# Seven products in place of eight for the last two groups of the second layer

## The chip, the cores and the metric

The kernel runs on one core of a Trainium2 chip. The metric is the device time of one execution in microseconds; lower is better. The kernel before took 1112.73 us in the median of three runs (1112.61 to 1113.55).

## The reference

```
# attention: 4 batches x 8 heads, 576 tokens, head size 64; only scores within tau of a row's maximum count
x  = attn_out.transpose(0, 2, 1, 3).reshape(2304, 512)
# first layer
h = x @ w_in1                                  # [2304, 2048]
g = where(h >= 1, h, where(h <= -1, 0, (h + 1)**2 / 4))
x = g @ w_out1                                 # [2304, 512]
# second layer
h = x @ w_in2                                  # the first product
g = h * clip(h + 3, 0, 6) / 6                  # the gate
return (g @ w_out2).astype(float32)            # the second product
```

All in float32. The change concerns the first product of the second layer alone.

## The kernel before

The tokens are taken in groups. In the second layer there are four groups of 512 tokens (0 to 3) and one of 256 (4). The 2048 hidden columns are taken in 16 blocks f of 128. Each float32 operand is split in two parts, a rounded one (hi) and the remainder (lo), and a product of two such operands takes three matmuls: hi by hi, hi by lo, lo by hi. The split of a tile is one copy on ScalarE (ACT) and one subtraction on VectorE (DVE) or GpSimd (POOL).

`dense` (L888) runs the second layer as a list of steps (group, f), 16 for each group. A step has the first product for this f (`em_h`, L710: four chunks of the 512 inputs by three terms, 12 matmuls of 512 columns, at L719), the gate (ReLU on ACT L732, minimum and product on DVE L733, copy to hi on ACT L736, remainder on POOL L737), and, two steps late (`MLAG`), the second product for the f of two steps before (`em_out`, L746: four blocks of tokens by three terms, 12 matmuls at L761, which add up over all f in a pair of PSUM banks). After the last f of a group `fin_out` (L814) copies the four blocks out, two on DVE (L819) and two on ACT (L817), and stores them. The first products turn through four PSUM banks, Q0 to Q3; the outputs use two pairs, P0 and P1. For the group of 256 tokens the first product has 256 columns and the second two blocks of tokens.

The inputs of a group come back from DRAM (`x2d`) through three buffers `xst` and are split in `split_x` (L674; L696 load, L699 hi, L700 lo); the program asks for them in steps 11 to 14 of the group before. The weights of the second layer are loaded through three buffers `w_raw` (L97, L100) and split while the first layer's last groups and group 3 run (`ahead3`, L1059); from then on all of them stay on the chip, in the tiles `wi` and `wo`. The order of the groups is 3, 0, 1, 4, 2 (L1064).

What each engine's queue holds in which order is fixed when the program is built: instructions written earlier have priority, and one that is not ready by the builder's model of time lets a later one pass. On the chip each queue runs in that order. All loads and stores here are issued from the queue of SP.

## Time and profile before

| | before |
|---|---|
| median of the runs, us | 1112.73 |
| lowest and highest run, us | 1112.61, 1113.55 |
| profiled execution, us | 1113.27 |
| its span, first to last instruction, us | 1111.5 |
| TensorE (PE) busy, us | 1080.1 |
| VectorE (DVE) busy, us | 590.5 |
| ScalarE (ACT) busy, us | 619.6 |
| GpSimd (POOL) busy, us | 449.3 |
| moved by DMA, MB | 84.26 |

Busy times are sums over the instructions of one profiled execution, the span is from its first to its last instruction, and the profiled execution's own time lies 1.8 us above the span. Every time below comes from that execution. PEld is TensorE's weight load, which overlaps with PE. A busy PE says that a matmul was under way, not that columns passed at the full rate; for the rate one counts matmuls in a stretch.

### The profile page before, as it was taken

How to read it: one execution, taken by the hardware profiler on the slowest of the kernel's cores; microseconds unless marked ns; L12 is line 12 of the kernel's file. 1: busy time of each engine (PE TensorE's matmuls, PEld its weight loads, DVE VectorE, ACT ScalarE, POOL GpSimd, SP SyncE). 2: the span in 40 equal slices, each digit the busy share in tenths (PEclk: the TensorE clock that was granted, in tenths of full speed). 3: DMA queues.
4: the chain of work that ended last, by engine and by line, in shares of the span. 5: the costliest groups of instructions: out<-in, count | busy, mean ns of one | idle time of the engine just before them, and what ended most of it. 6: DMA issues, size and time to landing. Idle time of an engine off the chain costs nothing.

```text
span 1111.5 us, 17816 instructions
## 1 busy us (share of the span) xinstructions
PE 1080.1 (97%) x6562; PEld 886.0 (80%) x6562; DVE 590.5 (53%) x1205; ACT 619.6 (56%) x1227; POOL 449.3 (40%) x390
## 2 busy tenths in 40 slices
PE   7988889999999999999999999999999999999998
PEld 5555567778888888888799888888888888898886
DVE  6889898975767766255437665557411111211111
ACT  5777886876667667455657766545422232333222
POOL 1133767732322222165627566667522222222221
PEclk9999899999999999999999999999999999999999
DMA  6455445333222120024323445433010110010001
GB/s 172 119 100 105 124 118 134 70 87 74 62 63 64 41 80 26 29 85 153 94 78 96 151 148 161 153 108 95 25 37 1 34 38 1 10 39 11 10 1 38
DMA packets 140614, 84.26 MB, mean 76 GB/s; under 512 B 99824, under 2 KB 123632, under 8 KB 140528
## 3 DMA queue, kind: packets, MB, share of 16 engines
q1 hardware_dynamic: 139184, 82.84, 27.1%
q8 instruction: 51, 0.84, 0.3%
q10 hardware_dynamic: 1344, 0.30, 0.1%
q14 instruction: 35, 0.29, 0.1%
HBM read 65.73 MB, written 17.37 MB: 75 GB/s over the span
## 4 chain that ended last, share of the span: by engine, by line
PE 79%; DVE 8%; ACT 4%; POOL 3%; issue 2%; DMA 2%; SPq 1%; DVEq 0%; POOLq 0%; ACTq 0%
PE Q L719 31%; PE P L761 25%; PE Q L781 6%; PE Q L476 6%; PE P L375 5%; PE Q L289 5%; DVE p L390 2%; DVE p L412 2%; POOL w_c L138 1%; DVE w_c L136 1%; ACT e L403 1%; SPq L228 1%; DVE r L730 1%; DVE xl L700 1%; POOL gl L737 1%
## 5 line engine op out<-in xcount | busy, mean ns | idle before, releaser
L737 POOL TENSOR_TENSOR gl<-r,gh 128x512 fp32r<-128x512 f32 (+1 forms) x190 | 204.5, 1077 | 462.4 <-ACT gh L736 451.1
L719 PE MATMUL Q<-xh,wih 128*128 128x512 f32 (+1 forms) x760 | 261.5, 344 | 2.5 <-DVE r L730 2.3
L719 PE MATMUL Q<-xl,wih 128*128 128x512 f32 (+1 forms) x760 | 256.9, 338 | 0.0
L719 PE MATMUL Q<-xh,wil 128*128 128x512 f32 (+1 forms) x760 | 256.8, 338 | 0.0
L733 DVE SCALAR_TENSOR_TENSOR r<-r,Q 128x512 f32<-128x512 f32 (+1 forms) x80 | 50.7, 634 | 249.5 <-ACT r L732 249.4
L736 ACT ACTIVATE gh<-r 128x512 fp32r<-128x512 f32 (+1 forms) x190 | 100.0, 527 | 125.3 <-PE P L761 52.2
L719 PEld LDWEIGHTS Q<-xh,wih 128*128 128x128 f32 x760 | 144.0, 189 | 25.8 <-DVE r L730 3.8
L719 PEld LDWEIGHTS Q<-xl,wih 128*128 128x128 f32 x760 | 144.0, 189 | 15.8
L719 PEld LDWEIGHTS Q<-xh,wil 128*128 128x128 f32 x760 | 143.8, 189 | 15.3
L732 ACT ACTIVATE r<-Q,three 128x512 f32<-128x512 f32 (+1 forms) x80 | 51.4, 643 | 144.1 <-PE Q L719 140.9
L412 DVE SCALAR_TENSOR_TENSOR p<-p,th,e 128x576 f32<-128x576 f32 x144 | 122.7, 874 | 16.0 <-ACT e L403 10.3
L403 ACT ACTIVATE e<-p,nm 128x576 f32<-128x576 f32 x144 | 109.4, 776 | 33.9 <-DVE p L390 33.0
L730 DVE SCALAR_TENSOR_TENSOR r<-r,Q 128x256 f32<-128x256 f32 (+1 forms) x110 | 54.9, 499 | 123.5 <-ACT r L729 118.3
L289 PE MATMUL Q<-ident,p 128*128 128x128 f32 x656 | 106.6, 280 | 9.9 <-ACT Gf L440 7.1
L761 PE MATMUL P<-woh,gh 128*128 128x512 f32 x288 | 111.9, 390 | 0.6 <-DVE ob L819 0.6
L761 PE MATMUL P<-wol,gh 128*128 128x512 f32 x288 | 112.2, 390 | 0.0
L761 PE MATMUL P<-woh,gl 128*128 128x512 f32 x288 | 111.0, 390 | 0.0
L138 POOL TENSOR_TENSOR w_c<-w_c,w_raw 128x512 int32<-128x512 int32 x64 | 89.2, 1395 | 40.8 <-DVE w_c L136 21.5
L289 PEld LDWEIGHTS Q<-ident,p 128*128 128x128 f32 x656 | 73.8, 140 | 39.0 <-ACT Gf L440 13.0
L375 PE MATMUL P<-kt,qt 64*128 64x288 f32 (+2 forms) x508 | 84.1, 418 | 11.1 <-DVE p L390 9.2
L440 ACT ACTIVATE Gf<-Q 128x512 f32<-128x512 f32 x128 | 74.3, 596 | 16.3 <-PE Q L289 15.6
L728 ACT ACTIVATE r<-Q,half 128x256 f32<-128x256 f32 (+1 forms) x110 | 58.7, 535 | 33.4 <-PE Q L719 25.1
(106 smaller groups left out, 1960.7 us busy)
## 6 DMA issues: line engine op xcount, KB each, us to landing
w_raw<-in_moe_w_in_dram SPq DMA_DIRECT2D x32, 512.0 KB
w_raw<-in_moe_w_out_dram SPq DMA_DIRECT2D x32, 512.0 KB
vn<-in_v_dram SPq DMA_DIRECT2D x32, 128.0 KB
x2p<-ob SPq DMA_DIRECT2D x16, 256.0 KB
x2d<-ob SPq DMA_DIRECT2D x16, 256.0 KB
xst<-x2d SPq DMA_DIRECT2D x16, 256.0 KB
out_dram<-ob SPq DMA_DIRECT2D x16, 256.0 KB
xst<-xd SPq DMA_DIRECT2D x15, 256.0 KB
```

The lines of the kernel that those rows point to most:

```text
L138: x = G.tensor_tensor(out=c.bitcast(I32), in0=c.bitcast(I32), in1=r, op=ALU.add)
L289: x = T.transpose(out, in_, ident)
L375: mm = T.matmul(o, a[j][r, cs], w[j][r, k0:k0 + HS], start=(n == 0), stop=(n == len(terms) - 1), skip_group_check=True)
L403: pins["S"] = S.activation(out=e, in_=p[:, x], func=ACTF.Exp, bias=nm[:, x:x + 1], scale=-1.0)
L412: pins["M"] = V.scalar_tensor_tensor(out=p[:, x], in0=p[:, x], scalar=th[:, x:x + 1], in1=e, op0=ALU.is_le, op1=ALU.mult, accum_out=zt[j][ ...
L440: S.activation(out=f[:, h, :, d0:d0 + 128], in_=tm.rearrange("p (c n) -> p c n", c=4), func=ACTF.Copy)
L476: mm = T.matmul(o[h * D:(h + 1) * D], vn[j % 2][:, c, h, :], f[:, h, c] if c < 4 else t, start=(c == 0), stop=(c == 4), skip_group_check=True)
L719: mm = T.matmul(h, l[:, kk * 128:(kk + 1) * 128], r, start=(x == 0), stop=(x == 3 * KD - 1))
L736: x = S.activation(out=gh, in_=r, func=ACTF.Copy)
L737: y = G.tensor_tensor(out=gl, in0=r, in1=f32(gh), op=ALU.subtract)
L761: T.matmul(a, l, r, start=(first and x == 0), stop=(last and x == 2))
L781: mm = T.matmul(o, l, r, start=(f == fs[0] and x == 0 and i == 0), stop=(f == fs[-1] and x == 2 and i == 1), skip_group_check=True)
```

## The change

The order of the groups becomes 3, 0 in `dense` and then a new function `unit` for groups 1 and 2 together, with group 4 (`last`) woven into its end.

`unit` takes the f in pairs. For a pair, the first product of both groups is a product of two-by-two blocks: two halves of the 512 inputs, two f, two groups of tokens. Strassen's method (in Winograd's form) takes seven products of blocks for it in place of eight. Each has two chunks by three terms, 6 matmuls of 512 columns. It needs four sums of weight blocks (S1 to S4) for each pair and four of token blocks (T1 to T4), and on the results three copies to SBUF on ACT and four sums on DVE. Three of the products add onto a bank that holds an earlier one, after that one was copied out.

`combine` makes the sums of weights, splits them in hi and lo, and stores them with the plain blocks to DRAM (`sd`), for one pair in each of the steps 1 to 8 of group 0. It holds the sums in the buffers `pb` and `w_raw`. `prepare` loads the tokens of groups 1 and 2, makes their sums and splits them, in steps 11 and 12 of group 0; the parts take the tiles `wi` of f 0 to 13. `fetch` brings the weights of each product back from DRAM, 256 KB at a time, into twelve buffers that held the inputs of a group before.

In `unit`, the gates of group 1 go on to its second product, woven between the products of the next pair (`outs`). The gates of group 2 are stored to DRAM (`rd2`) and loaded and split again after the last pair (`again`); its second product comes last. In between, group 4 gets its weights back from DRAM (`fetch_rest`) and is woven into the second product of group 2.

The diff, cut to its core:

```diff
+    sd = [dram.tile([128, 8, 2, 256], F32, name=f"sd{p}") for p in range(KF // 2)]
+    rd2 = [dram.tile([128, MAIN], F32, name=f"rr{f}") for f in range(KF)]
...
+    def place_of(f, hl, dt, name):
+        return (wbase if f < NF1 else wpool[f]).tile([128, 512], dt, tag=f"wi{hl}{f}", name=name)
...
+            wide["t"] = ctx.enter_context(tc.tile_pool(name="tx", bufs=1, side="right"))
...
+    G1, G2 = 1, 2
+    order3 = [NB - 1, 0]
+    combos = {}
+    XN = ("B11", "B21", "T2", "T3", "T4", "T1", "B22")
+    PRODUCTS = tuple(zip(("A11", "A12", "S2", "S3", "A22", "S1", "S4"), XN))
+    WN = ("A11", "A12", "A21", "A22", "S1", "S2", "S3", "S4")
+    def halves(n, name):
+        return place_of(n, "h", F32R, name), place_of(n, "l", F32R, name)
+    def temps(c):
+        if c == 0:
+            return ([wide["p"].tile([128, MAIN], F32, tag="xst", name="tx", bufs=3) for _ in range(3)]
+                    + [wide["t"].tile([128, MAIN], F32, tag=f"t{x}", name="tx") for x in range(3)])
+        return ([wide["p"].tile([128, MAIN], F32, tag="pb", name="tx", bufs=KD) for _ in range(4)]
+                + [wide["t"].tile([128, MAIN], F32, tag=f"t{x}", name="tx") for x in (3, 4)])
+    def prepare(c):
+        b11, b21, b12, b22, t1, t2 = temps(c)
+        for t, g, kk in ((b11, G1, c), (b21, G1, 2 + c), (b12, G2, c), (b22, G2, 2 + c)):
+            nc.sync.dma_start(out=t, in_=x2d[g][:, kk, :])
+        def part(k, t):
+            hi, lo = combos[c, XN[k]] = halves(2 * k + c, "xw")
+            S.activation(out=hi, in_=t, func=ACTF.Copy)
+            E = G if k % 2 else V
+            E.tensor_tensor(out=lo, in0=t, in1=f32(hi), op=ALU.subtract)
+        def minus(o, x, y):
+            V.tensor_tensor(out=o, in0=x, in1=y, op=ALU.subtract)
+        part(0, b11)
+        part(1, b21)
+        minus(t1, b12, b11)
+        minus(t2, b22, t1)
+        part(2, t2)
+        minus(b12, b22, b12)
+        part(3, b12)
+        minus(b11, t2, b21)
+        part(4, b11)
+        part(5, t1)
+        part(6, b22)
+    ring = []
+    RING = [f"x{hl}{kk}" for kk in range(3) for hl in "hl"]
+    got = {}
+    def fetch(p, w):
+        t = wide["x"].tile([128, 2, 2, 128], F32R, tag=RING[len(ring) % 6], name="sw", bufs=2)
+        ring.append(t)
+        nc.sync.dma_start(out=f32(t), in_=sd[p][:, WN.index(w)].rearrange("p x (k n) -> p x k n", k=2))
+        got[p, w] = t
+    turn_of = {}
+    def ringed(tag, dt):
+        k = turn_of[tag] = turn_of.get(tag, -1) + 1
+        first, extra = {"r": (2, ("t3", "t4")), "gh": (3, ("t1",)), "gl": (3, ("t2",))}[tag]
+        k %= first + len(extra)
+        if k < first:
+            return wide["g"].tile([128, MAIN], dt, tag=tag, name=tag, bufs=first)
+        return wide["t"].tile([128, MAIN], dt, tag=extra[k - first], name=tag)
+    def gate(src):
+        r = ringed("r", F32)
+        S.activation(out=r, in_=src, func=ACTF.Relu, bias=three)
+        V.scalar_tensor_tensor(out=r, in0=r, scalar=6.0, in1=src, op0=ALU.min, op1=ALU.mult)
+        return r
+    def parts(r):
+        gh, gl = ringed("gh", F32R), ringed("gl", F32R)
+        S.activation(out=gh, in_=r, func=ACTF.Copy)
+        G.tensor_tensor(out=gl, in0=r, in1=f32(gh), op=ALU.subtract)
+        return gh, gl
+    def outs_of(g, accs, i, f, hl):
+        if i % 2 == 0 and f == 0:
+            accs[i // 2] = pair_bank(f"P{i // 2}")
+        a = accs[i // 2][:, i % 2]
+        gh, gl = hl
+        wh, wl = wsp["o", 1, f]
+        c = slice(i * 128, (i + 1) * 128)
+        for x, (l, r) in enumerate(((gh[:, c], wh), (gh[:, c], wl), (gl[:, c], wh))):
+            T.matmul(a, l, r, start=(f == 0 and x == 0), stop=(f == KF - 1 and x == 2))
+        if f == KF - 1:
+            fin_out(g, a, i)
+    def unit():
+        accs, gg = {}, {}
+        for p in range(KF // 2):
+            def product(k, role, first=True):
+                w, x = PRODUCTS[k]
+                if (p, w) not in got:
+                    fetch(p, w)
+                t = got.pop((p, w))
+                if first:
+                    banks[role] = bank(f"Q{(p + role) % 4}")
+                y = 0
+                for c in range(2):
+                    xh, xl = combos[c, x]
+                    for l, r in ((0, xh), (0, xl), (1, xh)):
+                        T.matmul(banks[role], t[:, l, c, :], r, start=(first and y == 0), stop=(y == 5),
+                                 skip_group_check=True)
+                        y += 1
+                if p + 1 < KF // 2:
+                    fetch(p + 1, w)
+                return banks[role]
+            banks = {}
+            def copy(name, x):
+                t = wide["p"].tile([128, MAIN], F32, tag="pb", name=name, bufs=KD)
+                S.activation(out=t, in_=x, func=ACTF.Copy)
+                return t
+            def add(name, x, y, op=ALU.add):
+                t = place_of(14 + (name[2] == "2"), "hl"[name[1] == "2"], F32, name)
+                V.tensor_tensor(out=t, in0=x, in1=y, op=op)
+                return t
+            def outs(i):
+                if p:
+                    for f in (2 * p - 2, 2 * p - 1):
+                        outs_of(G1, accs, i, f, gg[f])
+            def store(r, f):
+                nc.sync.dma_start(out=rd2[f], in_=r)
+            f0, f1 = 2 * p, 2 * p + 1
+            p1 = copy("p1", product(0, 0))
+            gg[f0] = parts(gate(add("C11", product(1, 1), p1)))
+            outs(0)
+            u2 = copy("U2", product(2, 0, False))
+            outs(1)
+            u3 = copy("U3", product(3, 0, False))
+            c21 = add("C21", u3, product(4, 2), ALU.subtract)
+            gg[f1] = parts(gate(c21))
+            store(gate(add("C22", product(5, 3), u3)), f1)
+            if f1 < KF - 1:
+                outs(2)
+            c12 = add("C12", product(6, 3, False), u2)
+            store(gate(c12), f0)
+            if f1 == KF - 1:
+                outs(2)
+            outs(3)
+        hh = {}
+        def again(f):
+            r = ringed("r", F32)
+            nc.sync.dma_start(out=r, in_=rd2[f])
+            hh[f] = parts(r)
+        for f in range(2):
+            again(f)
+        fetch_rest(0)
+        fetch_rest(1)
+        tails = last()
+        next(tails)
+        for i in (0, 2, 1, 3):
+            for f in (KF - 2, KF - 1):
+                outs_of(G1, accs, i, f, gg[f])
+        accs = {}
+        for f in range(KF - 2):
+            again(f + 2)
+            for i in range(KD):
+                if f:
+                    next(tails, 0)
+                outs_of(G2, accs, i, f, hh[f])
+            if f in (1, 3):
+                fetch_rest(2 + f // 2)
+        for _ in tails:
+            pass
+        for i in (0, 2, 1, 3):
+            for f in (KF - 2, KF - 1):
+                outs_of(G2, accs, i, f, hh[f])
+    rest_w, rest_x = {}, []
+    def fetch_rest(k):
+        if k == 0:
+            for c in range(2):
+                t = wide["p"].tile([128, 2, GRP], F32, tag="xst", name="xst", bufs=3)
+                nc.sync.dma_start(out=t, in_=x2d[NB][:, 2 * c:2 * c + 2, :])
+                hi, lo = (place_of(14 + c, hl, F32R, "xw").rearrange("p (k n) -> p k n", k=2) for hl in "hl")
+                S.activation(out=hi, in_=t, func=ACTF.Copy)
+                V.tensor_tensor(out=lo, in0=t, in1=f32(hi), op=ALU.subtract)
+                rest_x.append((hi, lo))
+        for n in range(8 * k, 8 * k + 8):
+            if n < 28:
+                t = place_of(n // 2, "hl"[n % 2], F32R, "sw").rearrange("p (x k n) -> p x k n", x=2, k=2)
+            else:
+                t = wide["x"].tile([128, 2, 2, 128], F32R, tag=RING[n - 28], name="sw", bufs=2)
+            nc.sync.dma_start(out=f32(t), in_=sd[n // 4][:, n % 4].rearrange("p x (k n) -> p x k n", k=2))
+            rest_w[n // 2, n % 2] = t
+    def last():
...
+            h = bank(f"Q{f % 2}")[:, 0:GRP]
+            y = 0
+            for kk in range(KD):
+                t = rest_w[f, kk // 2]
+                xh, xl = (x[:, kk % 2, :] for x in rest_x[kk // 2])
+                for l, r in ((0, xh), (0, xl), (1, xh)):
+                    T.matmul(h, t[:, l, kk % 2, :], r, start=(y == 0), stop=(y == 11))
+                    y += 1
+            r = wide["p"].tile([128, GRP], F32, tag="xst", name="r", bufs=3)
+            S.activation(out=r, in_=h, func=ACTF.Relu, bias=three)
+            V.scalar_tensor_tensor(out=r, in0=r, scalar=6.0, in1=h, op0=ALU.min, op1=ALU.mult)
+            hl = gg[f] = wide["p"].tile([128, 2, GRP], F32R, tag="pb", name="gt", bufs=KD)
+            S.activation(out=hl[:, 0, :], in_=r, func=ACTF.Copy)
+            G.tensor_tensor(out=hl[:, 1, :], in0=r, in1=f32(hl[:, 0, :]), op=ALU.subtract)
+            yield
+            if f >= 2:
+                for i in range(2):
+                    outs(f - 2, i)
+            yield
+        for f in (KF - 2, KF - 1):
+            for i in range(2):
+                outs(f, i)
+    def combine(p):
+        f0, f1 = 2 * p, 2 * p + 1
+        ex = []
+        for n, f in enumerate((f0, f1)):
+            hi, lo = wsp["i", 1, f]
+            t = wide["p"].tile([128, 512], F32, tag="pb", name="ex", bufs=KD)
+            V.tensor_tensor(out=t, in0=f32(hi), in1=f32(lo), op=ALU.add)
+            ex.append(t)
+            for x, w in enumerate((hi, lo)):
+                nc.sync.dma_start(out=sd[p][:, 2 * n:2 * n + 2, x, :], in_=f32(w).rearrange("p (s n) -> p s n", s=2))
+        (a11, a12), (a21, a22) = ((t[:, 0:256], t[:, 256:512]) for t in ex)
+        s = [wide["p"].tile([128, 512], F32, tag="pb", name="ws", bufs=KD) for _ in range(2)]
+        (s1, s2), (s3, s4) = ((t[:, 0:256], t[:, 256:512]) for t in s)
+        for o, x, y, op in ((s1, a21, a22, ALU.add), (s2, s1, a11, ALU.subtract),
+                            (s3, a11, a21, ALU.subtract), (s4, a12, s2, ALU.subtract)):
+            V.tensor_tensor(out=o, in0=x, in1=y, op=op)
+        for n, t in enumerate(s):
+            z = stage.tile([128, 2, 512], F32R, tag="w_raw", name="wz", bufs=RAW)
+            S.activation(out=z[:, 0, :], in_=t, func=ACTF.Copy)
+            V.tensor_tensor(out=z[:, 1, :], in0=t, in1=f32(z[:, 0, :]), op=ALU.subtract)
+            for x in range(2):
+                nc.sync.dma_start(out=sd[p][:, 4 + 2 * n:6 + 2 * n, x, :],
+                                  in_=f32(z[:, x, :]).rearrange("p (s n) -> p s n", s=2))
     def ahead3(n, g, f):
         weights.half()
         weights.half()
         weights.upto(2 * KF + 2 * n + 2)
-    order3 = [NB - 1, *range(NB - 2), NB, NB - 2]
+        if g == order3[-1]:
+            if 1 <= f <= KF // 2:
+                combine(f - 1)
+            if f in (11, 12):
+                prepare(f - 11)
     dense(0, 2, seq2, fin_whole, ahead2, [(1, order3[0], 3)], rest)
     dense(1, 3, [(g, f) for g in order3 for f in range(KF)], fin_out, ahead3, [])
+    unit()
```

## Rows read from the trace of the kernel before

**Rows 1.** The page: its head and part 1.

```profile
span 1111.5 us, 17816 instructions
...
PE 1080.1 (97%) x6562; PEld 886.0 (80%) x6562; DVE 590.5 (53%) x1205; ACT 619.6 (56%) x1227; POOL 449.3 (40%) x390
```

**Rows 2.** Waits of PE, 700 to 1111 us: waiter, releaser, us, times, longest.

```profile
PE P L761 <- DVE ob L819: 0.6, 1, 0.6
```

**Rows 3.** Busy us of PE, PEld, DVE, ACT, POOL by stretch; clock, DMA share, GB/s.

```profile
505.00:510.00 5.00, 5.00 (x24) 4.14 (x23) 5.00 (x9) 4.02 (x9) 2.15 (x2) 1.00 0.93 290
455.00:460.00 5.00, 5.00 (x44) 5.00 (x43) 0.42 (x1) 3.10 (x9) 1.29 (x2) 1.00 0.17 56
776.00:800.00 24.00, 24.00 (x107) 19.72 (x106) 11.76 (x16) 12.19 (x21) 14.06 (x11) 1.00 0.08 23
800.00:844.00 44.00, 44.00 (x196) 36.44 (x195) 7.01 (x11) 12.29 (x19) 10.95 (x10) 1.00 0.08 28
888.00:976.00 88.00, 88.00 (x401) 73.30 (x401) 15.12 (x24) 24.71 (x39) 20.72 (x17) 1.00 0.05 15
1020.00:1107.80 87.80, 87.22 (x384) 71.55 (x382) 12.92 (x19) 22.19 (x34) 20.66 (x16) 1.00 0.04 9
```

**Rows 4.** Chain of waits: start us, length us, what.

```profile
821.36 4.99 PE P L761 x22
...
979.82 3.11 PE Q L719 x26
```

**Rows 5.** Timeline of PE: two starts of a first product.

```profile
795.13 0.39 PE L719 MATMUL Q<-xh,wih 128*128 128x512 f32 x1
...
882.17 0.39 PE L719 MATMUL Q<-xh,wih 128*128 128x512 f32 x1
```

**Rows 6.** Groups by shape, 888 to 976 us: busy, mean ns, idle before.

```profile
L737 POOL TENSOR_TENSOR gl<-r,gh 128x512 fp32r<-128x512 f32 x16 | 20.7, 1292 | 67.4 <-ACT gh L736 67.4
...
L733 DVE SCALAR_TENSOR_TENSOR r<-r,Q 128x512 f32<-128x512 f32 x15 | 10.3, 689 | 60.8 <-ACT r L732 60.7
L732 ACT ACTIVATE r<-Q,three 128x512 f32<-128x512 f32 x15 | 10.3, 689 | 36.9 <-PE Q L719 35.8 <-POOL gl L737 0.9
L736 ACT ACTIVATE gh<-r 128x512 fp32r<-128x512 f32 x15 | 9.5, 633 | 18.1 <-PE P L761 10.8 <-DVE r L733 7.3
L700 DVE TENSOR_TENSOR xl<-xst,xh 128x512 fp32r<-128x512 f32 x4 | 2.7, 693 | 4.1 <-ACT xh L699 4.1
```

**Rows 7.** Groups by shape, 804.88 to 891.9 us.

```profile
L700 DVE TENSOR_TENSOR xl<-xst,xh 128x256 fp32r<-128x256 f32 x4 | 1.7, 424 | 2.9 <-ACT xh L699 2.9
```

**Rows 8.** Timeline of SP's queue: start us, us, what.

```profile
455.68 0.38 SPq L795 DMA_DIRECT2D x2p<-ob  x1
...
502.93 1.29 SPq L696 DMA_DIRECT2D xst<-xd  x3
504.26 1.85 SPq L802 DMA_DIRECT2D pb<-x2p  x4
506.83 6.18 SPq L696 DMA_DIRECT2D xst<-xd  x4
...
621.88 0.32 SPq L812 DMA_DIRECT2D x2d<-ob  x1
...
772.10 0.33 SPq L100 DMA_DIRECT2D w_raw<-in_moe_w_out_dram  x1
```

**Rows 9.** Timeline of the end.

```profile
1103.99 1.29 DVE L819 TENSOR_SCALAR ob<-P 128x512 f32<-128x512 f32 x2 [3.74 <-PE P L761]
...
1104.74 0.50 PE L761 MATMUL P<-woh,gh 128*128 128x512 f32 x1 [0.56 <-DVE ob L819]
...
1107.39 0.39 PE L761 MATMUL P<-woh,gl 128*128 128x512 f32 x1
1107.81 0.60 ACT L817 ACTIVATE ob<-P 128x512 f32<-128x512 f32 x1 [0.78 <-PE P L761]
```

**Rows 10.** Groups by shape, 560 to 795 us.

```profile
L136 DVE SCALAR_TENSOR_TENSOR w_c<-w_raw,w_c 128x512 uint32<-128x512 uint32 x32 | 38.2, 1193 | 1.0
```

More of the change, by code (lines that the diff above doesn't have):

```diff
@@ new lines, in last, with outs @@
+    def last():
+        a, gg = {}, {}
+        def outs(f, i):
+            if f == 0:
+                a[i] = bank(f"Q{2 + i}")
+            hl = gg[f]
+            wh, wl = wsp["o", 1, f]
+            c = slice(i * 128, (i + 1) * 128)
+            for x, (l, r) in enumerate(((hl[:, 0, c], wh), (hl[:, 0, c], wl), (hl[:, 1, c], wh))):
+                T.matmul(a[i], l, r, start=(f == 0 and x == 0), stop=(f == KF - 1 and x == 2))
+            if f == KF - 1:
+                fin_out(NB, a[i], i)
+        for f in range(KF):
+            h = bank(f"Q{f % 2}")[:, 0:GRP]
[20 more added lines that the diff above has]
+                outs(f, i)
```

## Prediction

> **What bounds the kernel now.** I read the page first: TensorE (PE) is busy for 97% of the span [rows 1]. Then the waits of PE from 700 us on, which holds the whole second layer: the list is one wait of 0.6 us [rows 2]. Then the busy time by stretch: from 776 us on every stretch has PE busy for its whole length at a granted clock of 1.00, but for 0.58 us in the last, while VectorE (DVE), ScalarE (ACT) and GpSimd (POOL) are busy for 7.0, 12.3 and 11.0 of 44 us [rows 3]. So in the part that the diff touches only TensorE's own work counts, and everything else is free until it makes TensorE wait. The chain of waits gives the price of that work: 22 matmuls of 512 columns in 4.99 us, 0.2268 us each; 26 of 256 columns in 3.11 us, 0.120 us each [rows 4]. (The 389 ns that a group of matmuls shows is the time through the pipeline, not the spacing.) The first product of group 0 starts at 795.13 us and that of group 1 at 882.17 us [rows 5]: 87.04 us for 16 x 24 matmuls, 0.2267 us each. I use that.
>
> **What goes.** Before, groups 1 and 2 take 16 f x 12 matmuls each for the first product, 384. After, each of 8 pairs of f takes seven products of 2 chunks x 3 terms, 42 matmuls: 336. All have 512 columns and 128 x 128 weights as now. 48 matmuls x 0.2267 = 10.88 us less. The second products (192 matmuls for each of the two groups) and the last 256 tokens (192 of 256 columns, 96 of 512) keep their count; they only change place.
>
> **What comes, in the order of time.**
>
> Sums of weights (`combine`, for each of 8 pairs of f, written into eight steps of group 0). DVE gets two sums of 512 columns, four of 256 and two subtractions of 512: 4 x 0.693 + 4 x 0.424 = 4.5 us [rows 6, 7]; with the gate's 0.69 that is 5.2 us in a step of 24 matmuls, 5.44 us. ACT gets 2 x 0.63. This fits, and a gate may be late: its chain is 0.69 + 0.69 + 0.63 + 1.29 = 3.3 us [rows 6], and its reader starts four half steps, 10.9 us, after the product ends, so 7.6 us are to spare. I take 0; the other end is in the second rival.
>
> Its stores: 8 x 256 KB for each pair, 64 in all, 16.8 MB, on SP's queue, where a store took the queue 0.32 us [rows 8]: 20 us of 87. The queue holds little else there now. On the DMA engines a stretch with one such store (at 455.68 us, rows of 1 KB) shows a share of 0.17 of 5 us at 56 GB/s, so 280 KB in 0.85 us, 330 GB/s at full load; five busy us, with eleven loads of 256 KB issued, show 290 GB/s at a share of 0.93 [rows 3, 8]. So 51 to 58 us are needed, and group 0 lasts 87 us. The sums need not sit in the eight steps where they are written: the order on each queue is made when the program is built, by what is ready. The split of the last 256 tokens shows it: written into steps 11 to 14 of group 1 (942 to 964 us), its four pieces have run before 891.9 us [rows 7]. The last weights are loaded at 772.10 us [rows 8], after which the `w_raw` buffers that the sums use come free. I take 0.
>
> By the Trainium skill's "DMA: Bandwidth & Descriptors" (Bandwidth), transfers should be batched to 1 MiB: its table has 138 GB/s for 64 KB and 341 GB/s for 1 MB, so transfers of 256 KB would lie between, and the stores would take 49 to 122 us as an estimate, against 87. The trace disagrees with the slow end, 290 GB/s from loads of 256 KB [rows 3]. By its slow end the time would be that of the second rival; the chance stands there.
>
> Parts of the tokens (`prepare`, twice): 8 loads, and for each of the two chunks 8 passes on DVE (5.5 us by 0.69), 7 on ACT (4.4 us) and 3 on POOL (3.9 us). The last of them wait for the first product of steps 12 and 13 of group 0 (about 863 and 869 us), since they take the weights' place. Behind them on ACT and POOL stand the gates of those steps; 3.9 us are within the 7.6 us. The reader, the first of the seven products, comes at 882.17 + 5.44 = 887.6 us. I take 0.
>
> Start of the seven products. The first weights can be fetched as soon as their sums are stored, well before 887.6 us. If a fetch stood behind the last output store, TensorE would wait for a DMA; the end of the program shows that delay: the last piece of output starts at 1107.81 us, takes 0.60, and the span ends at 1111.5, so 3.1 us [rows 9, 1]. Bounds 0 and 3.1; I take 0, by the early split in rows 7.
>
> Waits between the small products. A bank that is copied out and then added to costs, from the last matmul's start, 0.39 + 0.03 + 0.60 (ACT) or 0.69 (DVE) + 0.05 to the next [rows 6, 9]; less the 0.23 of that matmul itself, 0.8 to 0.9 us of other work are needed in between. Six matmuls are 1.36 us. In a pair, product 1 and six output matmuls lie ahead of product 2, six ahead of product 3: covered. Product 6 is tighter: ahead of its bank's release stand the subtraction for C21 and perhaps its min-and-multiply on DVE; with both, the bank is free about 2.9 us after product 4 ends, and 2.72 us of work lie between. Up to 0.2 us, seven times. The first pair has no output matmuls; there product 3 meets an uncovered copy, 0.8 us, and product 6 another, unless product 4 or the next pair's first is put ahead. Bounds 0 and 1.4 + 1.7 us; I take 0.5, as in rows 2 such waits were filled with other matmuls but for one.
>
> The step to the last groups. After product 6 of the last pair, 12 + 24 output matmuls of group 1 are ready, 8.2 us. The 256-token group needs its tokens split into the tiles of C12, which are free after add, ReLU and multiply (2.1 us), then 0.63 + 0.69: 3.5 us, and weights whose loads wait only for products 0 and 1. The reload of group 2's gates needs a load and 0.63 + 1.29. Bounds 0 and about 3.1 us (one DMA in the open); I take 0.5. After that POOL has 1.29 us for each 2.72 us of outputs, and the end is as before.
>
> Loads in this part: 7 x 256 KB weights and 2 stores for each pair, 2.4 MB in 15 us, 157 GB/s, half of what rows 3 show. ACT has 3 x 0.60 + 4 x 0.63 + 2 x 0.63 = 5.6 us and DVE 8 x 0.69 = 5.5 us in 15 [rows 6, 9]. I take 0.
>
> **Sum.** The profiled execution took 1113.27 us; 1113.27 - 10.88 + 1.0 = 1103.4. The median of the runs is 0.54 below that execution, so 1102.9 us.
>
> **Rivals.**
> 1. The seven products don't stay dense. A product has 6 matmuls where a step had 12, and every second one waits for a copy; the order of each engine is fixed when the program is built, and if a gate's instruction is put ahead of a copy, TensorE waits the whole 0.8 us. For: the 0.56 us for which a matmul waits at the end on the copy of the other half of its pair of banks [rows 9]. Against: it is the only one [rows 2]. Price: 0.8 us in each of 8 pairs, 6.4 us, or one in each of two places at the borders, 3.1 us each: 1106 to 1109, say 1107.5 us.
> 2. The stores pace the kernel: slower than before. ACT writes the parts of the sums into `w_raw`, three buffers; when those wait for their stores, the gates behind on ACT wait too. At 290 GB/s a pair takes 7.2 us against 5.44, 14 us over eight pairs, less the 7.6 us to spare: 6.7 us lost, 1109.6 us, still faster. It decides from 18.5 us on, 7.75 us for a pair, 271 GB/s; at 240 GB/s it is 8.7 us a pair, 18.8 us lost, 1121.7 us. DVE could pace in the same way: a pass that takes 0.69 us alone took 1.19 us in the mean beside POOL's weight work [rows 10], which would make 4.5 us 7.7 and a step 8.4. For: rows 3 are near the deciding rate. Against: the sums can spread over 87 us, and POOL is busy for a quarter of it.
> 3. The work doesn't shrink as it says: the borders and the pairs together (3.1 + 3.1 + 3.1 + 1.4 us at their upper ends) eat the 10.88 us. 1112.5 us, no change.
>
> The Trainium skill's "GPSIMD Engine Reference" states (Specifications) that GpSimd's SBUF interfaces are shared with VectorE, with contention when a DVE instruction has two SBUF inputs. The 1.19 us agrees with it. By it alone the sums, which all have two such inputs, would make eight steps of group 0 3.0 us too long each, 24 us less the 7.6, and the time 1119 us, with the second rival's chance.
>
> **Chances.** Forecast 0.62, its own range 1101.3 to 1104.8; first rival 0.24; second 0.08, of which 0.06 slower than before; third 0.06, of which 0.03 within 0.2% (2.2 us, about what this kernel's runs can tell from no change) and the rest split. Faster 0.88, same 0.05, slower 0.07. The lower end is the saving with no loss and without the 0.6 us wait: 1113.27 - 10.88 - 0.6 - 0.54 = 1101.3. The upper end takes in the first rival whole and stops short of the second's dear part: 1108.5.
>
> **What would show it.** 48 PE matmuls fewer on the page; TensorE's waits after 888 us of about 1 us in sum, none over 1 us; the spacing of matmuls at 0.2267 us; no wait of ACT for a store's buffer between 776 and 880 us that lasts beyond 7 us; the fetches of the first pair issued before 880 us. It is wrong if PE is idle for over 3 us after 795 us, or if a stretch of group 0 takes over 5.44 us a step.

## The result: slower, and the profile after

The changed kernel took 1120.56 us in the median of six runs (1119.25 to 1121.4), the kernel before, run beside it on the same chip, 1113.09 us (1112.61 to 1113.55): a ratio of 1.0066, 95% interval 1.0053 to 1.0079. The forecast was 1102.9 us with a range of 1101.3 to 1108.5. The profiled execution took 1121.24 us, 7.97 us more than the one before.

The page after, part 1 (busy us, share of the span, instructions): the 48 matmuls are gone from PE's count, so the change does what it says, and yet the span [rows 1] is 7.6 us longer. DVE has 64 us more to do.

```profile
span 1119.1 us, 18317 instructions
PE 1076.2 (96%) x6514; PEld 879.5 (79%) x6514; DVE 654.7 (59%) x1307; ACT 642.0 (57%) x1271; POOL 464.2 (41%) x396
```

The waits of PE from 600 us on (waiter, releaser, us in total, times, longest). Before, the list from 700 us on was one wait of 0.6 us [rows 2]. Now it is led by the remainder of the gate, `gl`, which POOL makes (L742, L737 before).

```profile
PE P L766 <- POOL gl L742: 7.9, 6, 2.7
PE P L766 <- DVE ob L812: 1.7, 1, 1.7
PE P L766 <- ACT gh L741: 0.8, 1, 0.8
PE P L766 <- ACT ob L822: 0.8, 1, 0.8
PE P L1150 <- DVE ob L824: 0.5, 1, 0.5
PE P L1150 <- POOL gl L1139: 0.2, 1, 0.2
PE Q L1170 <- DVE C L1186: 0.2, 1, 0.2
```

The first four, 11.2 us, are in group 3 and the start of group 0 (L766 is the second product of `dense`); only the last three, 0.9 us, are in the seven products or behind them. Busy time by stretch says the same (columns as in [rows 3]). The seven products start at 900.8 us, and PE is full from 888 to 976 us; 776 to 844 us, full before with DVE at 7.01 of the last 44 us, has lost 7.6 us of PE, and DVE is at 37.

```profile
776.00:800.00 24.00, 22.01 (x94) 17.03 (x92) 20.20 (x28) 12.12 (x21) 14.53 (x11) 1.00 0.48 154
800.00:844.00 44.00, 38.41 (x152) 30.40 (x153) 37.02 (x61) 20.34 (x35) 19.29 (x11) 0.92 0.70 233
888.00:976.00 88.00, 88.00 (x390) 72.88 (x389) 27.45 (x41) 31.38 (x51) 15.46 (x12) 1.00 0.48 157
...
800.00:810.00 10.00, 7.82 (x26) 5.74 (x26) 10.00 (x18) 3.84 (x8) 5.56 (x3) 0.83 0.61 199
810.00:820.00 10.00, 7.35 (x25) 5.97 (x26) 9.40 (x17) 4.12 (x8) 4.08 (x2) 0.83 1.03 353
```

The balance: from 720 to 888 us the trace has 676 matmuls where before had 750, 74 fewer, which is 16.8 us at 0.2267. Of these 11.2 us are the waits; between 800 and 820 us, where the longest of them lie, the granted clock is 0.83, so for a part of the time at the lower of its two levels (1.2 of 2.4 GHz), and 51 matmuls take 15.17 busy us where they need 11.56, 3.6 us more. The other 2.0 of the 16.8 us are not placed. So 10.88 us were gained behind 888 us, 16.8 lost ahead of it, and 0.9 lost in and behind the seven products: +6.8. Of the remaining 1.1 us of the 7.97, 0.6 is there before any of the new work has run: a first product that started at 689.80 us starts at 690.43. The rest is open.

The same comparison of starts says where the 16.8 us were lost. The first product of the last step of group 3 starts at 796.73 us instead of 789.69, 7.04 us late, and that of the second step of group 0 at 816.62 instead of 800.57, 16.05 us late. So 6.4 us (7.04 less the 0.63 from the start) were lost ahead of 797 us, and 9.0 in the 20 us behind.

What DVE does there shows in the groups by shape, 720 to 888 us (busy us, mean ns, idle before). The sums of weights (L1311, L1320, L1324) run from 719 to 831 us, with passes of the token parts (L1096) among them; until 801 us DVE and POOL also split the second layer's weights (until 790 before). The passes of 512 columns of these lines, with both inputs in SBUF, take 825 to 938 ns in the mean, against 693 for such a shape [rows 6], POOL's `gl` 1559 against 1292 [rows 6] (1355 before in this same stretch); passes with one input in PSUM (L738, L812) take 680, as ever.

```profile
L742 POOL TENSOR_TENSOR gl<-r,gh 128x512 fp32r<-128x512 f32 x28 | 43.7, 1559 | 54.2 <-ACT gh L741 51.3 <-DVE ws L1320 1.9 <-PE Q L724 1.0
L738 DVE SCALAR_TENSOR_TENSOR r<-r,Q 128x512 f32<-128x512 f32 x28 | 18.9, 679 | 23.5 <-ACT r L737 23.5
L1324 DVE TENSOR_TENSOR wz<-ws,wz 128x512 fp32r<-128x512 f32 x16 | 14.9, 938 | 4.9 <-ACT wz L1323 4.9
L1311 DVE TENSOR_TENSOR ex<-wih,wil 128x512 f32<-128x512 f32 x16 | 13.1, 825 | 0.0
L1096 DVE TENSOR_TENSOR tx<-tx 128x512 f32<-128x512 f32 x8 | 6.7, 862 | 5.7 <-DMA tx<-x2d 5.7
L812 DVE TENSOR_TENSOR ob<-P,pb 128x512 f32<-128x512 f32 x3 | 2.0, 681 | 0.0
```

The longest wait, piece by piece, from the timelines of DVE, POOL, ACT and PE, 798 to 813 us (start, length, what, idle before in brackets). The gate's ReLU starts at 800.77 and takes 0.67; its next step on DVE (L738) is ready at 801.44 and runs at 805.84, behind seven passes of the sums, 4.4 us late. Then `gl` starts on POOL at 807.26 and takes 5.34 us instead of 1.29: DVE runs one two-input pass after the other, and the last 1.29 us of POOL's 5.34 begin at 811.31, about when DVE reaches a pass with an operand in PSUM (811.39). TensorE has waited 2.69 us. From the start of ReLU to the end of `gl` it is 11.8 us; I had 3.3 with 7.6 to spare.

```profile
800.77 0.67 ACT L737 ACTIVATE r<-Q,three 128x512 f32<-128x512 f32 x1
801.12 1.70 POOL L742 TENSOR_TENSOR gl<-r,gh 128x512 fp32r<-128x512 f32 x1
801.63 1.75 DVE L1311 TENSOR_TENSOR ex<-wih,wil 128x512 f32<-128x512 f32 x1
803.30 0.68 DVE L1324 TENSOR_TENSOR wz<-ws,wz 128x512 fp32r<-128x512 f32 x1
803.90 0.75 DVE L1320 TENSOR_TENSOR ws<-ex 128x256 f32<-128x256 f32 x2
804.57 0.41 DVE L1320 TENSOR_TENSOR ws<-ws,ex 128x256 f32<-128x256 f32 x1
804.91 0.68 DVE L1311 TENSOR_TENSOR ex<-wih,wil 128x512 f32<-128x512 f32 x1
805.51 0.41 DVE L1320 TENSOR_TENSOR ws<-ex,ws 128x256 f32<-128x256 f32 x1
805.84 0.67 DVE L738 SCALAR_TENSOR_TENSOR r<-r,Q 128x512 f32<-128x512 f32 x1
806.55 0.63 ACT L741 ACTIVATE gh<-r 128x512 fp32r<-128x512 f32 x1
807.26 5.34 POOL L742 TENSOR_TENSOR gl<-r,gh 128x512 fp32r<-128x512 f32 x1 [4.44 <-ACT gh L741]
811.39 0.67 DVE L738 SCALAR_TENSOR_TENSOR r<-r,Q 128x512 f32<-128x512 f32 x1
812.65 0.80 PE L766 MATMUL P<-woh,gl 128*128 128x512 f32 x1 [2.69 <-POOL gl L742]
```

The Trainium skill's "SBUF — State Buffer" (Who interferes with whom) says that a DVE instruction with two SBUF inputs contends with a GpSimd instruction that reads SBUF, that the shared port pair is an exclusive lock, and that the order of issue decides who blocks. The trace agrees that the two contend and that either can lose: POOL in the 5.34 us above, where it lost to several DVE passes in a row, and DVE in the 1.75 us of L1311 at 801.63, which started while `gl` ran until 802.82.

The token parts cost in another way. In the chain that ended last (start us, length us, what), a load of tokens follows a store of the same `x2d`, and DVE's pass for it (L1096) waits at the head of its queue for that load; the addition that ends a block of the first layer's output (L812) stands behind it, and TensorE waits 1.68 us for that.

```profile
727.22 2.92 DMA x2d<-ob
730.16 2.94 DMA tx<-x2d
...
734.05 1.76 DVE tx L1096
735.81 0.61 DVE ob L812
```

### The profile page after: what moved, and what is told of

The parts are those of the page before. It is cut to its first block, busy times and chain, and to the rows that moved or that the text cites. A ratio compares the mean times of both kernels' runs of the same rounds, so it can differ in the third digit from the quotient of the medians.

```text
span 1119.1 us, 18317 instructions
## 1 busy us (share of the span) xinstructions
PE 1076.2 (96%) x6514; PEld 879.5 (79%) x6514; DVE 654.7 (59%) x1307; ACT 642.0 (57%) x1271; POOL 464.2 (41%) x396
## 4 chain that ended last, share of the span: by engine, by line
PE 75%; DVE 13%; ACT 4%; POOL 3%; issue 2%; DMA 2%; SPq 0%; DVEq 0%; ACTq 0%; POOLq 0%
PE Q L724 20%; PE P L766 13%; PE P L1150 7%; PE Q L786 7%; PE Q L1170 7%; PE Q L481 6%; PE P L380 6%; PE Q L294 5%; DVE p L395 2%; PE Q L1276 2%; PE Q L1287 2%; DVE p L417 2%; DVE w_c L141 1%; DVE w_c L135 1%; DVE w_c L132 1%
## 5 line engine op out<-in xcount | busy, mean ns | idle before, releaser
L742 POOL TENSOR_TENSOR gl<-r,gh 128x256 fp32r<-128x256 f32 (+1 forms) x142 | 156.7, 1104 | 283.3 <-ACT gh L741 269.4
L724 PE MATMUL Q<-xh,wih 128*128 128x256 f32 (+1 forms) x568 | 193.8, 341 | 2.6 <-DVE r L735 2.4
L724 PE MATMUL Q<-xl,wih 128*128 128x256 f32 (+1 forms) x568 | 189.2, 333 | 0.0
L724 PE MATMUL Q<-xh,wil 128*128 128x256 f32 (+1 forms) x568 | 189.0, 333 | 0.0
L741 ACT ACTIVATE gh<-r 128x256 fp32r<-128x256 f32 (+1 forms) x142 | 73.0, 515 | 81.5 <-DVE r L735 31.1
L1139 POOL TENSOR_TENSOR gl<-r,gh 128x512 fp32r<-128x512 f32 x32 | 41.6, 1301 | 137.4 <-ACT gh L1138 122.9
L1170 PE MATMUL Q<-xw,sw 128*128 128x512 f32 x336 | 80.7, 389 | 0.2 <-DVE C L1186 0.2
L395 DVE TENSOR_SCALAR_CACHE_REDUCE p<-P 128x576 f32<-128x576 f32 x90 | 65.2, 750 | 19.9 <-PE Q L294 12.0
L786 PE MATMUL Q<-gh,woh 128*128 128x256 f32 x240 | 75.4, 314 | 1.4 <-DVE ob L799 1.4
L1170 PEld LDWEIGHTS Q<-xw,sw 128*128 128x128 f32 x336 | 63.0, 188 | 13.5 <-DVE C L1186 0.4
```

The costliest lines, as they stand in the source:

```text
L395: reads(V.tensor_scalar(out=p[:, x], in0=s[:, :, 0:HS], scalar1=taus[:, 3:4] if j >= JR else -1.0, scalar2=3e38, op0=ALU.mult, op1=ALU.min ...
L724: mm = T.matmul(h, l[:, kk * 128:(kk + 1) * 128], r, start=(x == 0), stop=(x == 3 * KD - 1))
L742: y = G.tensor_tensor(out=gl, in0=r, in1=f32(gh), op=ALU.subtract)
L786: mm = T.matmul(o, l, r, start=(f == fs[0] and x == 0 and i == 0), stop=(f == fs[-1] and x == 2 and i == 1), skip_group_check=True)
L1170: T.matmul(banks[role], t[:, l, c, :], r, start=(first and y == 0), stop=(y == 5), skip_group_check=True)
```

## The experiments

Four theories stood at the start; the letters are those of the expectations. Early passes (A, later D): the sums' DVE passes, which the builder lets run early, beside the weight split, hold up the gates. Amount (B): the sums are too much for a step wherever they stand. Early loads (C): the token parts' loads, waited for on DVE, start the loss. Stores (S): the sums' stores and buffers do it (the prediction's second rival). The undoing uses `after` (L105), with which the kernel already pins the weight split: an instruction may not be placed ahead of the given one in its engine's queue; `pins["V"]` is the last gate's pass on DVE.

**Both kept where they are written.**

```diff
 # combine
-            V.tensor_tensor(out=t, in0=f32(hi), in1=f32(lo), op=ALU.add)
+            after(V.tensor_tensor(out=t, in0=f32(hi), in1=f32(lo), op=ALU.add), pins["V"])
 # prepare
-            S.activation(out=hi, in_=t, func=ACTF.Copy)
+            after(S.activation(out=hi, in_=t, func=ACTF.Copy), pins["S"])
-            V.tensor_tensor(out=o, in0=x, in1=y, op=ALU.subtract)
+            after(V.tensor_tensor(out=o, in0=x, in1=y, op=ALU.subtract), pins["V"])
```

> The first DVE operations of the sums of weights, and the first ACT and DVE operations of the token parts, are ordered behind the gate of the step before the one where they are written, so they can't run ahead of group 0. Theory A (place): the loss of the changed kernel, about 18 us between 720 and 840 us, comes from these operations running early, beside the split of the second layer's weights; held back they cost TensorE next to nothing: 1103 to 1106 us, group 0's end near 888 us. Theory B (amount): a pair's sums (5.2 us of DVE with the gate, 7.2 us of stores at 290 GB/s) are too much for a step of 5.44 us wherever they stand: 1109 to 1116 us, with TensorE's waits moved into 800 to 850 us.

**Only the token parts kept; only the sums kept** (the second and the first half of that edit).

> Only the token parts are held back to steps 11 and 12 of group 0; the sums of weights still run early. Theory A: this gives back what DVE lost while it stood before a load of tokens (5.9 us near 727 and 3.6 us near 827 us in the chain of waits), 2 to 4 us of TensorE: 1116 to 1119 us. Theory C (one blocked load starts the whole loss, the weight split then runs behind from 730 us on): nearly all comes back, 1104 to 1108 us. Theory B: no change, 1120 us.

> Only the sums of weights are held back to steps 1 to 8 of group 0; the token parts may run early. Theory A: most comes back, 1104 to 1108 us. Theory B: 1110 to 1118 us, as the same work meets the same step length. Theory C: little comes back, 1116 to 1120 us.

**The sums left out.**

```diff
-            V.tensor_tensor(out=t, in0=f32(hi), in1=f32(lo), op=ALU.add)
...
+        for y in (0, 4):                       # the plain blocks are stored twice
+            for n, f in enumerate((f0, f1)):
+                for x, w in enumerate(wsp["i", 1, f]):
+                    nc.sync.dma_start(out=sd[p][:, y + 2 * n:y + 2 * n + 2, x, :], ...)
```

> The sums of weights are left out: in their places plain blocks of weights are stored, so the result is another, but the number and size of the stores, the fetches and the seven products are as in the changed kernel. DVE and ACT have no pass for sums, and no store holds a w_raw buffer. Theory A and any theory in which DVE's passes or the wait for w_raw cost the time: 1103 to 1107 us. If the stores themselves (16.8 MB early, on the same DMA engines as the weights) cost it: 1112 us or more.

Measured, each against the kernel before on the same chip (where runs of different chips are compared below, it is by the ratio):

| | median, us | ratio | 95% interval |
|---|---|---|---|
| both kept | 1106.88 | 0.9937 | 0.9923 to 0.9952 |
| token parts kept, sums early | 1118.91 | 1.0043 | 1.0029 to 1.0057 |
| sums kept, token parts early | 1107.70 | 0.9948 | 0.9933 to 0.9962 |
| no sums, token parts early | 1112.09 | 0.9984 | 0.9975 to 0.9994 |

Early sums cost 12 us (1118.91 against 1106.88), early token parts 1 to 3 by the ratios (0.9948 against 0.9937, 1.0066 against 1.0043), which the intervals do not tell from nothing. Theory B falls with the first kernel: kept in place, the sums hold DVE for 19.59 of 20 us and TensorE loses nothing. So a full DVE is not the cost by itself, and POOL has about as many passes there (3) as in the changed kernel (4). What differs is that a gate's step on DVE starts at most 1.9 us after its ReLU there (814.31, the ReLU at 811.72 taking 0.69) where the changed kernel had 4.4, and that no `gl` takes over 1.86 us where it had 5.34. The first kernel, 800 to 820 us:

```profile
800.00:820.00 20.00, 20.00 (x90) 16.57 (x89) 19.59 (x36) 8.89 (x15) 4.50 (x3) 1.00 0.64 212
```

The last run missed its expectation of 1103 to 1107. Its list of waits of PE shows why: without the sums an output behind the early token loads is waited for longer, not shorter.

```profile
PE P L766 <- DVE ob L812: 4.6, 1, 4.6
PE P L766 <- POOL gl L742: 1.0, 1, 1.0
```

To see that it was this, the same with the token parts kept:

> The kernel without sums (plain blocks stored in their places, so the result is another) had 1112.1 us where theory A had 1103 to 1107; its trace shows one wait of TensorE of 4.6 us at 720 to 740 us for an output on DVE, which stood behind a token load, and the clock at 0.92 after it. This run is the same with the token parts held back to steps 11 and 12 of group 0. If that blocked load is the whole of it: 1103 to 1106 us and no wait in 700 to 800 us. If the early stores slow something else: over 1108 us.

1104.55 us, ratio 0.9916 (0.9901 to 0.9930): the 4.6 us wait is gone and 7.5 us with it. So the early loads do cost. The size is not explained: with the sums kept and the loads early this wait is 1.7 us, as in the changed kernel. In the kernel without sums three passes of L1096 run straight ahead of L812 (734.19 to 739.28 us), in the other two kernels two.

**Passes or stores.** Both with the token parts kept and the sums' work early; one makes the sums and does not store them, the other stores and does not make them.

```diff
 # first: no store, the fetch reads plain blocks
-            for x in range(2):
-                nc.sync.dma_start(out=sd[p][:, 4 + 2 * n:6 + 2 * n, x, :], ...)
 # second: no DVE pass, ACT copies the plain blocks into w_raw, stored as in the change
+            for x, w in enumerate(wsp["i", 1, f]):
+                S.activation(out=z[:, x, :], in_=f32(w), func=ACTF.Copy)
```

> As with the token parts held back (1118.9 us), and the sums of weights early, but the sums are not stored: the fetches for them read plain blocks, so the result is another, and 8.4 MB of stores and every wait of a w_raw buffer for a store are gone. The loss against the kernel with both held back is 12 us. Theory D (DVE's passes beside POOL's split of the weights cost it): at least 8 of the 12 us stay, 1114 to 1119 us. Theory S (the stores and the buffers that they hold cost it): 1106 to 1109 us.

> The mirror of the run before: token parts held back, no DVE pass for sums at all (the sums are left out; ACT copies plain blocks into w_raw, four passes for a pair instead of two, and they are stored from there as in the changed kernel). Theory D: 1106 to 1109 us. Theory S: 1114 to 1119 us. In between: both have a share, and the two runs' losses over 1106.9 us give them.

Without the sums' stores (those of the plain blocks remain) 1119.73 us (1.0057, 1.0042 to 1.0072), as slow as with them; with stores and without passes 1106.79 (0.9942, 0.9928 to 0.9957). The kernel without sums and with its token parts kept also has all 64 stores, at 0.9916. The stores fall as a cause, the early passes stand; the copies of ACT into `w_raw` may cost up to 3 us (0.9942 against 0.9916, intervals that overlap a little).

**Half of the sums kept** (pairs 4 to 7; the line is that of the first experiment with `pins["V"] if p >= 4 else None`).

> Token parts held back; the sums of pairs 4 to 7 held back to their steps, those of pairs 0 to 3 free to run early. All held: 1106.9 us, none held: 1118.9 us. Theory D (each early pass beside the split of the weights costs its share): about half of the 12 us, 1111 to 1114 us. If only the crowd at the end costs (all eight pairs in 790 to 820 us, with DVE busy all the time): 1107 to 1109 us.

1114.13 us (1.0005, 0.9995 to 1.0014): half of the pairs cost 0.0068 of the 0.0106 between all early and none, so the cost grows with the early passes and is no single event.

**Is it the second SBUF input?**

```diff
-            V.tensor_tensor(out=t, in0=f32(hi), in1=f32(lo), op=ALU.add)
+            V.tensor_scalar(out=t, in0=f32(hi), scalar1=1.0, scalar2=None, op0=ALU.mult)
...             # the same for L1320 and L1324; in the second run each such line stands twice
```

> As e2_hold_tokens, sums early, in the same place in the queues, with the same stores, but each of the eight DVE passes of a pair's sums has one SBUF input in place of two (it copies one operand, so the sums are left out). Slowdown theory (the cost of the early sums comes from DVE passes with two SBUF inputs and POOL's passes slowing each other): the passes take 0.69 us or less, POOL's gl pass 1.3 to 1.4 us instead of 1.6, most of the 12 us goes: 1107 to 1111 us. Order theory (eight more passes ahead of a gate in DVE's queue cost the same whatever they take): 1116 to 1119 us. Between, 1111 to 1116: both have a part.

> As e11, but each one-input pass of the sums is issued twice, so that DVE's queue is held about as long as in e2_hold_tokens or longer, without a second SBUF input (the sums are left out). If the time for which DVE's queue is held decides, 1115 to 1120 us. If it is POOL, slowed by the second input, whose late gl passes make TensorE wait, it stays near e11, 1107 to 1111 us, with gl at 1.3 to 1.4 us.

One input once: 1111.69 us (0.9983, 0.9974 to 0.9992). Twice: 1119.38 (1.0056, 1.0039 to 1.0073). In groups by shape, 720 to 888 us, the first with single passes:

```profile
L742 POOL TENSOR_TENSOR gl<-r,gh 128x512 fp32r<-128x512 f32 x30 | 41.6, 1387 | 68.6 <-ACT gh L741 68.5
L1320 DVE TENSOR_SCALAR ws<-ex 128x256 f32<-128x256 f32 x24 | 9.5, 421 | 0.0
L1311 DVE TENSOR_SCALAR ex<-wih 128x512 f32<-128x512 f32 x15 | 8.5, 595 | 0.1
L1324 DVE TENSOR_SCALAR wz<-wz 128x512 fp32r<-128x512 f32 x16 | 7.3, 456 | 8.2 <-ACT wz L1323 8.2
L1320 DVE TENSOR_SCALAR ws<-ws 128x256 f32<-128x256 f32 x8 | 3.0, 378 | 0.1
```

The sums' lines hold DVE for 28 us with single one-input passes, 49 with the two-input ones, 55 with doubled ones; the time over the kernel with both kept is 0.0046, 0.0106 and 0.0119 of the time before, 5, 12 and 13 us. So among kernels whose passes run early the cost goes with the time for which they hold DVE. That time alone does not decide: from 776 to 844 us DVE is busy for 51.02 of 68 us with both kept and TensorE loses nothing, while with single passes DVE is busy for 37.25 and TensorE loses 4.8. So it counts whether the passes stand ahead of the gates or behind them. 800 to 820 us, with single passes and then with the two-input ones (tokens kept):

```profile
800.00:820.00 20.00, 17.29 (x74) 13.38 (x73) 13.83 (x33) 11.04 (x19) 5.42 (x4) 1.00 1.02 342
800.00:820.00 20.00, 17.91 (x66) 14.30 (x67) 19.91 (x35) 7.63 (x13) 9.08 (x4) 0.85 0.87 289
```

With single passes POOL is hardly slower than before, 1387 ns in the mean against 1355 and at most 1.75 us in both kernels, and 5 us are lost all the same: most of these come from the queues of DVE and ACT (whose copies also run early), not from a slower POOL. A part of the step from 5 to 12 us is the clock: the 66 matmuls of the second row take 17.91 busy us where 14.96 are needed, at a granted clock of 0.85, the 74 of the first 17.29 where 16.78 are, at 1.00. The one-input pass is no clean control, though: it too took up to 1.53 us beside POOL where it takes 0.41 alone, and in the doubled run a `gl` took 4.41. How much of the rest is plain place in the queue and how much the two engines slowing each other stays open; in the one wait taken apart above, it is 3.3 us of the one (4.4 less the 1.07 by which L1311 was longer) and 5.1 of the other.

**The rest of the saving.** With both kept, 7.0 of the 10.88 us were back. In that kernel the token parts collide as well (groups by shape, 840 to 888 us):

```profile
L1093 POOL TENSOR_TENSOR xw<-tx,xw 128x512 fp32r<-128x512 f32 x6 | 10.3, 1738 | 0.0
L1093 DVE TENSOR_TENSOR xw<-tx,xw 128x512 fp32r<-128x512 f32 x8 | 10.3, 1314 | 1.2 <-ACT xw L1091 1.2
```

So next POOL's six of these passes (three for each `prepare`) went to DVE, and in a further kernel the second batch of weights for group 4 was also fetched a step later, since PE loses 1.2 us at 1000 to 1016 us with the DMA engines full.

```diff
-            E = G if k % 2 else V
-            E.tensor_tensor(out=lo, in0=t, in1=f32(hi), op=ALU.subtract)
+            V.tensor_tensor(out=lo, in0=t, in1=f32(hi), op=ALU.subtract)
 # the further kernel
-        fetch_rest(1)
-            if f in (1, 3):
-                fetch_rest(2 + f // 2)
+            if f in (0, 2, 4):
+                fetch_rest(1 + f // 2)
```

> Sums and token parts held back as in the first run (1106.9 us), and the token parts' subtractions all on DVE, none on POOL. In the first run DVE's passes took 1.7 us beside POOL's in 856 to 872 us and TensorE waited 0.6 us for a gate's remainder on POOL; by theory D that wait goes and DVE's passes there come back to 0.69 us: 0.5 to 1 us faster, 1106 us. If sharing has no part in it: the same or slower, as DVE gets 4 us more.

> As the run before, and the second eight weight loads of the 256-token group are asked for one step later in the second product of group 2. In the first run TensorE waited 1.2 us between 1000 and 1016 us, where the DMA engines were full (share 1.04) and the reload of group 2's gates came late. If that load is the cause: 1 to 1.5 us faster than the run before, 1104.5 to 1105 us. If the waits there are those of the banks and gates: no change.

1103.96 us (0.9923, 0.9906 to 0.9940) and 1103.28 (0.9911, 0.9897 to 0.9926). With more work on DVE and less on POOL the passes now take 778 ns in the mean, and the wait of 0.6 us for a `gl` at 876 us is gone (groups by shape, 840 to 888 us, in the first of the two):

```profile
L1092 DVE TENSOR_TENSOR xw<-tx,xw 128x512 fp32r<-128x512 f32 x14 | 10.4, 778 | 0.1
```

With the weights fetched as before the time is 0.0014 lower by the ratio, 1.6 us, which the intervals do not tell from nothing. The later fetch shows nothing that can be told apart; the stretch it aims at is no fuller (PE 15.22 without it, 14.96 with it, of 16). Busy time by stretch of the last kernel:

```profile
888.00:1000.00 112.00, 112.00 (x496) 92.75 (x495) 39.35 (x59) 42.16 (x69) 19.30 (x15) 1.00 0.55 180
1000.00:1016.00 16.00, 14.96 (x80) 11.87 (x79) 7.41 (x13) 7.82 (x14) 4.81 (x5) 1.00 1.05 393
```

It is faster than the kernel before and the changed one: 9.9 us under the kernel before by the ratio, as much as the forecast's 10.88 less 1.0.

## Why the prediction was wrong

- **What goes** was right: 6514 matmuls, 48 fewer, and 888 to 1000 us is dense.
- **The sums of weights, "I take 0"** is the step that failed. It has two halves. The cost was worked out for eight steps of group 0, where DVE is nearly idle, and there no wait of TensorE came of it (the first experiment). Then I read the builder's freedom to run them early as a help, "The sums need not sit in the eight steps where they are written". It runs them as soon as it thinks them ready, from 719 us on, and in DVE's queue they stand ahead of gates. That "a gate may be late", with 7.6 us to spare, did not hold there: a chain of 3.3 us took 11.8. Of the loss 6.4 us (the wait of 1.7 for a token load among them) came beside the weight split, where DVE and POOL had 11.8 and 14.1 of 24 us to do [rows 3] and slow each other [rows 10], and more, 9.0, in the 20 us behind, where little but sums and gates was left on DVE. Measured as the price of running the sums early: 12 us.
- The evidence I gave for free early running, the split of the 256 tokens [rows 7], had run where DVE and POOL are slack. It said nothing about a stretch with gates close behind each other and other work in the queue.
- **The second rival** had a part of the mechanism in its one sentence on DVE, with the price of 1.19 us for a pass [rows 10], and its forecast by the shared ports, 1119 us, came nearest. I gave it 0.08 because it was counted for group 0, where POOL is busy for a quarter of the time: right for that place, but it is not where the work ran. That 1119 lies near 1120.56 is therefore luck: it was reckoned as DVE pacing group 0, and with the sums in group 0 the time was 1106.88 us. Its main form, the stores, did not occur: with all of them and no passes the time was 1104.55 us, and 1106.79 with those of the sums' places going through `w_raw`.
- **Parts of the tokens, "I take 0"**: 1 to 3 us by the difference of early and kept, 1.7 us of it seen as the wait for L812. I had looked at the gates behind them and not at DVE waiting for a load with the first layer's additions behind it.
- **Waits between the small products**, 0.5 us: 0.2 us, one wait of a product (L1170). The first rival did not occur. **The step to the last groups**, 0.5 us: 0.7 us, the two waits of L1150 in the list. In the kernels with both kept the two together are 0.8 to 1.2 us (PE 14.81 to 15.22 of 16 us at 1000 to 1016).
- The test "PE is idle for over 3 us after 795 us" fired: 5.6 us in 800 to 844 alone. So did the one on group 0: its first step took 10.0 us (806.62 to 816.62) where 5.44 were allowed.

## What to carry to other kernels

Before side work is costed at nothing, find out when the builder will run it, not where it is written: if it is ready early, it can come to stand ahead of urgent passes, and the price is read there. The engine's busy share does not give it: DVE at 51.02 of 68 us cost TensorE nothing with the sums behind the gates, and at 37.25 it cost 4.8 us with passes ahead of them. Work that must not run early is pinned behind the engine's last urgent instruction. What stands in an in-order queue ahead of a gate counts with its length as it is beside POOL's passes, and a wait for a load at its head counts for everything behind it.

## What the runs showed of the hardware

- A POOL pass of 1.29 us took 5.34 beside DVE passes that follow each other without a gap; in the two fastest kernels one took 7.03 us at 861.6 us, with no wait of TensorE for it. A DVE pass of 0.68 us took up to 1.80 beside POOL (L1311 with the token parts kept). The gate's DVE pass, with one operand in PSUM, stayed at 0.67 to 0.69 in all of these.
- A one-input DVE pass over SBUF was slowed beside POOL too, 0.41 to 1.53 us.
- In the 20 us in which PE waited 0.79, 1.75 and 2.69 us the granted clock was 0.83, and the 51 matmuls took 3.6 us more than at 0.2267 us each.
